# Row-tiled transposes of q and k into two PSUM banks, with a new order table, in a fused linear-attention and gMLP kernel

## The chip, the cores and the metric

The kernel runs on one core of a Trainium2 chip. The metric is device time in microseconds (us). A core has five engines that run side by side, each through its own instruction queue in order: TensorE (PE, with weight loads shown as PEld), VectorE (DVE), ScalarE (ACT), GpSimd (POOL) and SyncE (SP), which here issues the DMAs. Matrix products land in PSUM, eight banks of 128 partitions by 512 fp32 values.

## The reference

Two layers follow each other. The first is a gated linear attention over 4 batches, 8 heads, 768 positions and head size 48; the second a gated MLP with a spatial product.

```python
for t in range(S):                                   # attention, per batch b and head h
    state = alpha[:, :, t, :, None] * state + einsum('bhd,bhe->bhde', k[:, :, t], v[:, :, t])
    y[:, :, t] = einsum('bhd,bhde->bhe', q[:, :, t], state)
x = y.transpose(0, 2, 1, 3).reshape(B, S, H * D)     # 4 x 768 x 384
h = maximum(x @ w_in, 0)                             # 384 x 1024
u, v = h[..., :512], h[..., 512:]
v_n = (v - mean(v)) / sqrt(var(v) + 1e-6)            # over the last axis
v_s = einsum('ts,bsd->btd', w_spatial, v_n) + b_spatial[None, :, None]
out = (u * v_s) @ w_out                              # 512 x 384
```

## The kernel before

The 768 positions of a batch are cut into 6 chunks of 128, so there are 24 chunks, numbered `i` = 0 to 23. Inside a chunk the recurrence is turned into matrix products: cumulated logs of alpha (`cum`), k divided by and q multiplied with their exponentials (`kt`, `qt`), transposes of both (`trk`), masked scores (`sc`, then `m`), and the chunk's output `y` from scores times v and from q times the state of the chunk before. `upd`, `z`, `S` and `sb` carry the state on.

Chunks 0 to 7 are worked on as four pairs (`pair`), whose loads bring two chunks in one DMA of 384 KB. Chunks 8 to 23 are single (`first`), with loads of 192 KB. Each load is for one of alpha, k, q, v and is named `ac`, `kc`, `qc`, `vc`.

The second layer follows batch by batch: `xs`, `xt`, `xe` bring `y` into the transposed bf16 tile `xT`; `v` (`second_v`) and `u` (`second_u`) are the two halves of `x @ w_in`, `bn`, `rs`, `vn` normalise `v`, `s` is the spatial product (groups of six matmuls of 384 columns), `g` the gate, `o` the output product, `st` the store. The weights come in six loads of 768 KB: `w_in.1` (the half for `v`), `w_in.0`, `w_sp.0` to `w_sp.2`, `w_out`, each cast to bf16 by three or four `cast` operations.

All of this is first described as a list of operations with an engine, a cost for the planner and dependencies; nothing is issued at that time. The order comes from a planner and is written out as a string, `PLAN` (lines 57 to 107). A word such as `P474` says: operation 474 is issued now, on PE (`P`), DVE (`D`), ACT (`A`), POOL (`G`) or by SP (`S`; `Q` marks the end of its DMA). So the table fixes both the engine of each operation that has a choice and the order in each engine's queue. Numbers after colons are columns of extra matmuls on a constant tile `junk`, put in front of the operation; they compute nothing and keep PE active early in the run. `replay` (line 110) reads the table.

PSUM banks are handed out by `bank` in strict turn, eight of them. A bank that comes round again is written only when the engine that reads its last content has done so.

For a single chunk `tr_qk` (line 681) takes one bank as 128 x 1024 bf16 and fills it with eight transposes of 128 x 128: four of k (line 685) and four of q (line 687), each with the whole identity as the moving operand. One copy (`ev_qk`, lines 196 or 198, on ACT or DVE) brings the 128 x 1024 values to `kqT` in SBUF. The scores (line 717) use 48 rows of it, starting at row 0 or 64, so they already run as two row tiles, into two banks. Pair chunks have transposes of their own (line 480), which the change leaves alone.

Of the kernel before, what the change touches and what calls it, by code (L numbers as in the profile page):

```python
# [36 lines left out]
class Slot:  # L37
# [8 lines left out]
    "sb": {"POOL": 0.73, "DVE": 0.95},  # L46
    "vn": {"DVE": 0.42},
    "xe": {"ACT": 0.4},
    "ev": {"DVE": 0.61, "ACT": 0.91},
    "u": {"ACT": 0.39, "DVE": 0.49},  # L50
    "o": {"ACT": 0.4},
}
# [2 lines left out]
LETTERS = {"P": "PE", "D": "DVE", "A": "ACT", "G": "POOL", "S": "SP", "Q": "DMA"}  # L55

PLAN = """
G32 S34 Q33 S36 G0 S38 S94 Q35 D1 Q37 S40 A42 D2 Q39 S98 P43:512:512:192 P53:64 A44 A45 D46 Q95 S96 A54 A55 G56
P49:352 D57 Q41 D47 S100 P61:320 P59 D50 P51 A102 D62 D60 Q99 D52 S163 P241:352 P103 P113 A58 G48 P71 A104 P63 D72
Q97 A114 S165 A105 D65 A64 A115 D73 G66 A242 Q101 S167 D107 P74:512:160 D117 P111 G116 D106 A112 Q164 S169 P119:384  # L60
D75 P109 P121 A110 D68 D122 A120 G69 Q166 D76 S4 P131:352 A118 G108 D132 P134:128 G67 P123 D133 A171 Q168 S301 G70
D136 P77 A124 P172 D125 A78 P182 D135 A173 G126 Q170 P81 S9 P79 A183 P137 D128 G175 A82 D127 P138 A174 P83 G3 A184
Q5 S305 P142 A80 D176 A139 D185 G129 P180:320 A84 P178 P140 A143 D186 A177 G187 P144 D181 P190 A141 Q302 P188 D179
A145 P192 D191 A189 A6 G8 D194 D7 P200 Q10 P197 G130 S14 P146 D199 A309 S303 P88 D198 A147 D201 P85 A193 A89 G195
D202 P310 Q306 S307 A86 G196 P157 D90 A311 P203 A312 D148 A158 Q15 P204 P208 G12 P320 A205 D13 P243 A321 P206 D11
A209 D159 P153 S18 A207 P210 A322 P212 D314 Q304 S361 A211 D87 A160 P318 P215 G16 A213 D324 P221 Q308 G17 A216 D154
P151 A91 D319 G323 P225 S22 D217 A244 A222 Q19 S363 P231 G313 A226 D214 P227 A152 P149 A228 D162 P155 D92 A150 D232
P316 A218 P326 P229 Q362 A315 G325 S365 D327 P328 A317 D93 P223 D220 A156 Q23 P330 D329 S401 A224 D219 A230 P338 D20
G21 D332 A331 A369 P233 D161 G333 P341 D234 P235 G334 Q364 S405 D335 P245 D339 P253 G336 D340 Q366 P254 S403 G24
D342 P370 P257 Q402 G25 A371 D343 S436 P237 A372 A374 P258 D236 G373 Q406 D375 P239 S367 P246 G337 A240 Q404 P249  # L70
D247 S440 A238 P250 D255 G248 P377 Q437 A409 D259 S407 P269 A378 D251 G256 P270 Q368 S468 P410 D271 P344 A412 A411
Q441 P383 S438 A345 P348 G413 D385 P261 A349 Q408 P265 A414 S26 P346 D415 P262 A347 Q469 G376 D384 P350 S470 P266
G252 A351 P417 A444 Q439 S472 P379 G260 P386 D418 P445 A387 Q27 D380 P273 G416 S442 D263 A447 A446 P274 G272 D267
A449 P423 D450 P388 G381 P355 D275 A389 G382 P352 D425 G448 D424 Q471 P419 S563 P395 A353 P399 A476 G268 D354 Q473
A356 P426 S474 P397 G276 A400 D420 D357 A427 P452 Q443 S565 A396 G421 P477 P428 D453 P390 A478 G29 Q564 A429 S567
D31 G479 P458 D30 A398 P430 A28 D460 Q475 S595 G264 A480 P277 A431 D481 Q566 G422 P281 A391 S597 D459 A451 P483 Q568
A278 P285 S599 D484 A282 G482 A571 P461 D392 Q596 A286 S569 P485 A358 P454 P572 D455 A462 Q598 P289 D487 S601 A574
A573 G456 P463 D486 P393 G457 Q600 A464 S630 P293 A576 D432 G575 A290 P488 Q570 A294 D577 S634 P465 A489 D394 A603
P579 Q602 D359 S632 A466 P490 P604 D580 A433 P297 Q631 D360 A491 S670 D434 P585 A605 D435 P492 A606 A298 Q635 G607
D587 S706 A608 P505 A467 D609 P499 G578 Q633 S636 D586 A493 P501 A494 P611 D506 Q671 S674 P581 P588 A502 D582 P503  # L80
A500 D495 Q707 G583 P507 S738 A638 P515 G610 D612 Q637 A496 P639 S710 P511 A641 D497 A589 P613 D498 A640 Q675 P519
D584 S672 A643 P590 G642 P516 A504 D644 Q739 A591 P508 S708 D517 P512 D614 Q711 G518 P646 D509 S742 P520 D513 A647
G615 P527 Q673 D521 S832 G510 P617 A714 P652 D618 A678 Q709 P535 G514 S676 D619 P528 Q743 P679 G616 D529 S740 P531
A680 D653 P532 G522 A681 A683 Q833 S712 P715 D684 P620 G682 A716 P523 D654 Q677 A717 A719 S836 P536 G718 A746 P592
A645 Q741 D537 S864 A621 G530 P747 D533 A593 P655 D720 Q713 P622 S834 P686 A656 D594 A623 P524 Q837 A748 P648 S868
P657 A750 P722 D649 A687 D525 P624 G650 Q865 S744 D751 G651 P539 A658 D723 Q835 A840 S866 G538 P692 A540 P728 D694
A685 P659 Q869 G526 A625 S838 D693 P543 A660 G749 Q745 P688 S899 P547 A544 D689 A661 D729 P695 G690 Q867 S939 P662
D730 G691 A696 P753 A548 Q839 P697 A663 G721 S903 P841 D754 A698 P666 G534 A842 D626 Q900 P724 P731 S901 A872 P699
A843 A845 D725 Q940 D667 A732 G726 S870 P755 D846 A700 P664 G844 D756 A627 Q904 P733 S941 P551 A734 D757 G727 A665
P848 Q902 D629 A701 S974 G752 P873 D628 P735 D849 A874 Q871 P758 A552 S1006 D702 G876 P555 A759 Q942 A875 A877 S943  # L90
G847 P854 A556 P760 D878 P668 Q975 A761 D856 S905 P559 A703 A736 D855 P762 Q1007 S945 A907 D705 P880 A669 D704 P857
Q944 A763 D881 P908 S976 P774 A560 D737 A909 P768 Q906 S978 A910 A858 P850 G911 P788 D764 A912 Q946 P859 A947 P776
S980 G879 D851 A860 D913 P772 A765 G852 Q977 D769 P770 S1010 A775 G853 D767 P915 D766 Q979 P948 S561 D916 P792 A950
A949 P882 A773 P789 Q981 G951 S1008 A771 P777 D790 A952 P793 G914 Q1011 D883 S545 D778 P861 G884 D953 Q562 G885 P886
A862 S1012 D794 P921 Q1009 P780 S541 A982 D888 G779 A1014 P955 D887 P784 Q546 G791 A956 D922 P917 P785 Q1013 D918
P983 D923 P889 Q542 P781 A890 P796 A984 D782 A985 P891 A987 P797 G986 A954 D988 P924 A892 P804 D786 G919 A925 P1015
D863 G989 P957 P926 A1016 G795 P805 A927 D798 P961 A1018 D958 G1017 P928 D962 P990 D806 G959 P937 D963 G787 A991
P800 D1019 P801 G783 A929 D920 P1021 A938 G807 P992 D802 P893 A1022 D993 P964 G803 A894 P996 P1023 A965 D895 G994
P812 G1020 P966 D998 P808 G995 A967 D997 A896 P935 G960 P968 D898 A936 D1024 G799 A809 P816 D1025 A813 P999 S814
A817 D930 P931 A1000 S810 P1026 A969 S549 D932 P1001 Q815 P820 A1027 D970 A1002 Q811 P1028 P824 A1029 Q550 A971  # L100
P1003 A821 D973 P1038 A1004 S822 P1036 S291 A825 P1030 A1039 S279 D1037 Q823 S283 P1040 D972 A1031 Q292 D897 S287
P1042 D1005 A1041 Q280 P1044 S826 P1056 Q284 D1032 S295 P828 Q288 A1033 P1052 Q827 A829 D1034 P933 Q296 D1035 S830
P1064 A934 S553 P1045 A1043 S818 Q831 P1053 S299 P1057 Q554 S557 D1054 P1060 D1046 Q819 P1065 D1058 Q300 P1048 D1066
Q558 P1049 D1055 P1072 D1050 P1073 D1047 P1068 G1051 D1059 P1061 G1067 P1069 D1074 P1075 D1062 D1070 P1079 G1063
A1076 D1071 P1083 S1077 A1080 P1099 S1081 A1084 P1087 D1100 Q1078 S1085 P1095 S1101 A1088 Q1082 P1091 D1096 S1089
Q1086 S1097 A1092 Q1102 S1093 Q1090 Q1098 Q1094
"""


# [13 lines left out]
def kernel(  # L123
# [12 lines left out]
    nc = tc.nc  # L136
# [178 lines left out]
    def k_window(t, hp, first):  # L315

        return t[:, 3 * hp + first:3 * hp + first + 2, :].rearrange("p b d -> p (b d)")
# [285 lines left out]
    def first(i):  # L603
# [75 lines left out]
        hold = {}  # L679

        def tr_qk(_):
            pt = bank([128, 512])
            t = hold["t"] = pt.bitcast(BF16).rearrange("p (n t) -> p n t", n=8)
            for hp in range(HP):
                nc.tensor.transpose(t[:, hp, :], k_window(kt3, hp, 1), ident)  # L685
            for hp in range(HP):
                nc.tensor.transpose(t[:, HP + hp, :], qt[:, hp].rearrange("p s d -> p (s d)"), ident)  # L687

        def ev_qk(eng):
            st["kqT"] = work.tile([128, 2, HP, C], BF16, name="kqT", bufs=4).rearrange("p a h c -> p (a h) c")  # L690
            copy(eng, st["kqT"], hold["t"])

        sl = Slot(ring)
        op(("trk", i), "PE", 0.46, tr_qk, got(("kt", i), ("qt", i), ("y", i - WK)), prio=P + 5, take=sl, cols=1024)
        op(("ev", i), ENGINES["ev"], None, ev_qk, got(("trk", i), ("y", i - WK), ("sc", i - WK)),
           prio=P + 6, use=[sl])

        if not last:
            def upd(_):
                st["tp"] = bank([128, HP, D])  # L700
                for hp in range(HP):
                    for s in range(2):
                        nc.tensor.matmul(  # L703
                            out=st["tp"][:, hp, :], lhsT=k_window(kt3, hp, 2 - 2 * s),
                            rhs=st["vb"][:, 2 * hp + s, :], start=(s == 0), stop=(s == 1))

            st["sl_t"] = Slot(ring)
# [11 lines left out]
                        start=True, stop=True)  # L719

        sl0, sl1 = Slot(ring), Slot(ring)
        op(("sc", i), "PE", 0.34, sc, got(("ev", i)), prio=P + 7, take=[sl0, sl1], cols=384)

        def mk(s):
            def emit(_):
# [387 lines left out]
```

## Time and profile before

| | us |
|---|---|
| median of 5 runs | 146.99 |
| lowest, highest | 146.33, 149.19 |
| the profiled execution | 149.19 |
| its span, first to last instruction | 147.4 |
| busy: PE, DVE, ACT, POOL | 139.2, 122.4, 108.5, 84.9 |

The profile is of one execution, the slowest of the five. Its span is 1.8 us shorter than its time; the rest lies around the instructions. A matmul's length in it includes the pipeline's tail, so consecutive matmuls overlap in the rows, and the cost of one in a stream is the distance between two starts. A granted clock of 1.00 is full speed.

### The profile page before, as it was taken

The numbers are of one execution on the slowest core, as the hardware profiler recorded it, in microseconds if no ns is written. First come the engines' busy times: TensorE is split into PE (matmuls) and PEld (weight loads), VectorE is DVE, ScalarE is ACT, GpSimd is POOL, SyncE is SP. The second block draws the span as 40 slices with busy tenths as digits, with TensorE's granted clock in tenths as the row PEclk, the third lists the DMA queues.
The fourth block names the chain that finished last, engine by engine and source line by source line (L and its number), as shares of the span: only waits on it lengthen the run. The fifth ranks groups of instructions, "written<-read, shape, count | busy, mean of one in ns | idle before, by whom it ended". The sixth has DMA issues, their size and how long they took to land.

```text
span 147.4 us, 4462 instructions
## 1 busy us (share of the span) xinstructions
PE 139.2 (94%) x1700; PEld 90.5 (61%) x1713; DVE 122.4 (83%) x266; ACT 108.5 (74%) x268; POOL 84.9 (58%) x145
## 2 busy tenths in 40 slices
PE   7989989699999999999999999999999999999990
PEld 3546667255776776576666576666667576656560
DVE  6867997778998779989899897999987999575970
ACT  3456787679955976999995899999767697953051
POOL 6634655549248799844357969870694979000530
PEclk9999999789999999999999999999999999999999
DMA  4999999999999999999999998997995000479035
GB/s 115 266 261 261 265 244 336 257 318 290 319 168 207 141 272 165 197 192 171 195 190 172 189 177 155 206 188 146 196 226 139 4 0 2 165 271 342 29 139 184
DMA packets 88998, 28.61 MB, mean 194 GB/s; under 512 B 83728, under 2 KB 87440, under 8 KB 88976
## 3 DMA queue, kind: packets, MB, share of 16 engines
q1 hardware_dynamic: 88944, 28.32, 88.6%
q8 instruction: 13, 0.21, 0.7%
q14 instruction: 9, 0.07, 0.2%
q0 software_dynamic: 32, 0.00, 0.0%
HBM read 23.60 MB, written 4.72 MB: 192 GB/s over the span
## 4 chain that ended last, share of the span: by engine, by line
PE 76%; SPq 11%; DMA 6%; ACT 2%; DVE 1%; issue 1%; DVEq 0%; ACTq 0%
PE bank L791 54%; SPq L410 11%; DMA raw_w<-in_moe_w_in_dram 6%; PE bank L717 3%; PE bank L365 2%; PE bank L687 2%; PE bank L685 2%; PE bank L745 2%; PE bank L635 2%; PE bank L739 2%; PE bank L703 2%; PE bank L801 1%; PE bank L638 1%; PE bank L579 1%; PE bank L430 1%
## 5 line engine op out<-in xcount | busy, mean ns | idle before, releaser
L791 PE MATMUL bank<-w_spT,vn 128*128 128x384 bf16 x192 | 36.7, 326 | 0.0
L946 POOL TENSOR_TENSOR gT<-vsb,uT 128x384 bf16<-128x384 f32 x27 | 25.0, 940 | 15.9 <-DVE vsb L933 15.6
L791 PEld LDWEIGHTS <-vn 128*128 128x128 bf16 x192 | 17.0, 97 | 9.1 <-issue 0.2
L659 POOL TENSOR_TENSOR kt<-kc,binv 128x384 bf16<-128x384 f32 x16 | 14.6, 916 | 13.0 <-ACT bc L654 8.3
L728 DVE TENSOR_TENSOR ptm<-bank,mask 128x512 bf16<-128x512 f32 x32 | 20.9, 682 | 0.8 <-PE bank L717 0.8
L791 PE MATMUL bank<-w_in,xT 128*128 128x512 bf16 x59 | 18.2, 403 | 2.3 <-ACT w_in L196 1.2
L933 DVE TENSOR_TENSOR vsb<-bank,bsp_bc 128x384 f32<-128x384 f32 x31 | 16.2, 550 | 4.4 <-PE bank L791 4.2
L336 POOL TENSOR_TENSOR state<-state,bc 128x192 f32<-128x192 f32 x20 | 10.5, 525 | 15.0 <-DVE state L331 6.1
L791 PE MATMUL bank<-xT,w_in 128*128 128x384 bf16 x96 | 19.0, 326 | 0.1
L791 PE MATMUL bank<-w_out_sb,gT 128*128 128x384 bf16 (+1 forms) x100 | 18.6, 319 | 0.1
L852 DVE BATCH_NORM_STATS2 stats<-v_sb 128x6 f32<-128x512 bf16 x20 | 13.7, 683 | 2.1 <-ACT v_sb L202 2.1
L202 ACT ACTIVATE v_sb<-bank 128x512 bf16<-128x512 f32 x20 | 11.9, 601 | 3.0 <-PE bank L791 2.9
L196 ACT COPY xT<-bank 128x384 bf16<-128x384 bf16 x24 | 11.7, 494 | 2.1 <-PE bank L365 1.9
L196 ACT CAST x_sb<-bank 128x384 bf16<-128x384 f32 x24 | 11.7, 488 | 1.7 <-PE bank L745 1.4
L198 POOL CAST sbd<-state 64x192 bf16<-64x192 f32 x34 | 11.7, 345 | 1.8
L186 PE MATMUL bank<-junk 128*128 128x512 f32 (+7 forms) x26 | 11.7, 559 | 1.1 <-DVE junk L232 1.1
L198 DVE COPY kqT<-bank 128x512 bf16<-128x512 bf16 (+1 forms) x21 | 11.0, 544 | 1.8 <-PE bank L687 1.2
L791 PEld LDWEIGHTS <-gT 128*128 128x128 bf16 x100 | 9.0, 97 | 5.4 <-issue 0.2
L196 ACT COPY kqT<-bank 128x1024 bf16<-128x1024 bf16 (+1 forms) x11 | 9.0, 823 | 4.3 <-PE bank L687 2.5
L202 ACT ACTIVATE uT<-bank 128x384 bf16<-128x384 f32 x25 | 11.6, 494 | 0.4 <-PE bank L791 0.4
L791 PEld LDWEIGHTS <-w_in 128*128 128x128 bf16 x96 | 8.5, 97 | 4.9
L563 DVE TENSOR_TENSOR ptm<-bank,mask 128x512 bf16<-128x512 f32 x16 | 10.2, 682 | 1.2 <-PE bank L552 1.2
(126 smaller groups left out, 296.3 us busy)
## 6 DMA issues: line engine op xcount, KB each, us to landing
ac<-in_alpha_dram SPq DMA_DIRECT2D x16, 192.0 KB, 4.7
kc<-in_k_dram SPq DMA_DIRECT2D x16, 192.0 KB, 4.5
qc<-in_q_dram SPq DMA_DIRECT2D x16, 192.0 KB, 4.6
vc<-in_v_dram SPq DMA_DIRECT2D x16, 192.0 KB, 4.4
raw_w<-in_moe_w_spatial_dram SPq DMA_DIRECT2D x3, 768.0 KB, 5.9
out_dram<-raw_w SPq DMA_DIRECT2D x11, 192.0 KB, 2.1
out_dram<-o_sb SPq DMA_DIRECT2D x9, 192.0 KB, 2.0
ac<-in_alpha_dram SPq DMA_DIRECT2D x4, 384.0 KB, 6.2
```

The costliest lines, as they stand in the source:

```text
L186: nc.tensor.matmul(out=flat[:, 0:cols].rearrange("p (a b) -> p a b", a=4), lhsT=junk, rhs=junk[:, None, 0:n].to_broadcast([128, 4, n]), st ...
L196: nc.scalar.copy(out=out, in_=in_)
L198: ENG[eng].tensor_copy(out=out, in_=in_)
L202: nc.scalar.activation(out=out, in_=in_, func=AF.Relu)
L336: ENG[eng].tensor_tensor(out=st["state"], in0=st["state"], in1=st["bc"][:, :, None].to_broadcast([128, HP, D]), op=ALU.mult)
L410: nc.sync.dma_start(out=t.rearrange("p h a d -> p h (a d)"), in_=src[b, :, t0:t0 + 2 * C, :].rearrange("h (p a) d -> p h (a d)", a=2))
L659: ENG[eng].tensor_mul(out=k_blocks(kt3)[:, :, :, 0:D], in0=quad(st["kc"]), in1=st["binv"])
L728: nc.vector.tensor_tensor(out=st["ptm"][:, s], in0=st[f"pt{s}"], in1=mask4, op=ALU.mult)
L791: return lambda ps: nc.tensor.matmul(out=out(ps), lhsT=lhsT(), rhs=rhs(), start=start, stop=stop)
L852: nc.vector.bn_stats(out=stats, in_=d["v_sb"][:, tt, :])
L933: nc.vector.tensor_tensor(out=hold["vs"], in0=ps[:, 0:TH], in1=bsp_bc[:, th, :], op=ALU.add)
L946: ENG[eng].tensor_tensor(out=bt[b]["gT"][:, dsl, cols], in0=hold["vs"], in1=bt[b]["uT"][:, dsl, cols], op=ALU.mult)
```

## The change

The transposes of a single chunk are cut at partition 64. For each of the eight blocks, the upper 64 rows are transposed with the upper-left 64 x 64 of the identity into one bank, and the lower 64 rows with the lower-right part into a second bank. Each of the sixteen transposes has 64 moving columns and uses 64 of PE's rows. Each bank then holds 128 x 512 bf16 values, and one copy for each bank writes its half of the columns of `kqT`; the two copies are operations of their own, which may be on different engines. The scores wait for both.

```diff
-    "ev": {"DVE": 0.61, "ACT": 0.91},
+    "ev": {"DVE": 0.34, "ACT": 0.48},
...
         def tr_qk(_):
-            pt = bank([128, 512])
-            t = hold["t"] = pt.bitcast(BF16).rearrange("p (n t) -> p n t", n=8)
-            for hp in range(HP):
-                nc.tensor.transpose(t[:, hp, :], k_window(kt3, hp, 1), ident)
-            for hp in range(HP):
-                nc.tensor.transpose(t[:, HP + hp, :], qt[:, hp].rearrange("p s d -> p (s d)"), ident)
-
-        def ev_qk(eng):
-            st["kqT"] = work.tile([128, 2, HP, C], BF16, name="kqT", bufs=4).rearrange("p a h c -> p (a h) c")
-            copy(eng, st["kqT"], hold["t"])
-
-        sl = Slot(ring)
-        op(("trk", i), "PE", 0.46, tr_qk, got(("kt", i), ("qt", i), ("y", i - WK)), prio=P + 5, take=sl, cols=1024)
-        op(("ev", i), ENGINES["ev"], None, ev_qk, got(("trk", i), ("y", i - WK), ("sc", i - WK)),
-           prio=P + 6, use=[sl])
+            for r in range(2):
+                hold[r] = bank([128, 512]).bitcast(BF16).rearrange("p (n t) -> p n t", n=16)[:, 0:2 * HP, :]
+            for n in range(2 * HP):
+                hp = n % HP
+                for r in range(2):
+                    rows = slice(64 * r, 64 * r + 64)
+                    nc.tensor.transpose(
+                        hold[r][:, n, :],
+                        k_window(kt3[rows], hp, 1) if n < HP else qt[rows, hp].rearrange("p s d -> p (s d)"),
+                        ident[rows, rows])
+
+        sls = [Slot(ring), Slot(ring)]
+        op(("trk", i), "PE", 0.24, tr_qk, got(("kt", i), ("qt", i), ("y", i - WK)), prio=P + 5, take=sls, cols=512)
+        for r in range(2):
+            def ev_qk(eng, r=r):
+                if "kqT" not in st:
+                    st["kqT"] = work.tile([128, 2, HP, C], BF16, name="kqT", bufs=4).rearrange("p a h c -> p (a h) c")
+                copy(eng, st["kqT"][:, :, 64 * r:64 * r + 64], hold[r])
+
+            op(("ev", i, r), ENGINES["ev"], None, ev_qk, got(("trk", i), ("y", i - WK), ("sc", i - WK)),
+               prio=P + 6, use=[sls[r]])
...
-        op(("sc", i), "PE", 0.34, sc, got(("ev", i)), prio=P + 7, take=[sl0, sl1], cols=384)
+        op(("sc", i), "PE", 0.34, sc, got(("ev", i, 0), ("ev", i, 1)), prio=P + 7, take=[sl0, sl1], cols=384)
```

The table `PLAN` is replaced as a whole. Read through the list of operations it changes the order in every queue and the engine of some operations. The first 21 loads of SP's queue, before and after:

```
before: ac.0 kc.0 qc.0 ac.2 vc.0 qc.2 kc.2 vc.2 ac.4 kc.4 qc.4 vc.4 w_in.1 ac.6 w_in.0 qc.6 w_sp.0 kc.6 vc.6 w_sp.1 ac.8
after:  ac.0 ac.2 kc.0 qc.0 qc.2 vc.0 kc.2 ac.4 vc.2 qc.4 w_in.1 kc.4 w_in.0 vc.4 ac.6 w_sp.0 qc.6 kc.6 w_sp.1 vc.6 w_sp.2
```

PE's queue around the first dense product, and a stretch of single chunks:

```
before: y.3 tr.q.2.0 tr.k.2.0 xt.2 xt.3 tr.q.2.1 tr.k.2.1 updq.2 sc.2.1 sc.2.0 v.0.2 v.0.1 v.0.0 cump.3.0 v.0.3
after:  y.3 tr.q.2.1 xt.2 tr.q.2.0 v.0.1 xt.3 tr.k.2.1 tr.k.2.0 v.0.0 sc.2.1 sc.2.0 v.0.2 v.0.3 updq.2 u.0.2.0

before: trk.10 cum.11 xt.9 v.1.2 sc.10 v.1.3 o.0.0 o.0.1 trk.11 o.0.2 y.10 sc.11 upd.10 cum.12
after:  trk.10 o.0.2 o.0.1 sc.10 trk.11 v.1.3 u.1.1.0 cum.12 upd.10 y.10 sc.11 u.1.0.0 xt.10 o.0.3
```

Of the operations with a choice of engine, counted over the whole table:

| operation | before | after |
|---|---|---|
| `ev` of single chunks | 10 DVE, 6 ACT (whole) | 20 DVE, 12 ACT (halves) |
| `ev` of pairs | 11 DVE, 5 ACT | 7 DVE, 9 ACT |
| `u` evictions | 7 DVE, 25 ACT | 18 DVE, 14 ACT |
| `g` | 4 DVE, 27 POOL | 2 DVE, 29 POOL |
| `sb` | 3 DVE, 17 POOL | 2 DVE, 18 POOL |
| weight casts | 6 DVE, 2 ACT, 8 POOL | 3 DVE, 4 ACT, 9 POOL |
| `vb` of single chunks | 4 ACT, 12 POOL | 8 ACT, 8 POOL |

The matmuls on `junk` have 4,160 columns in all in both tables, in other places. On POOL the load of the spatial bias now follows the building of the masks.

## The prediction

> **What bounds the kernel now.** I read the page first, then the chain in order of time, then the windows by stage, and last TensorE's and SP's timelines around the changed step. From the page, busy times and the granted clock:
>
> ```profile
> PE 139.2 (94%) x1700; PEld 90.5 (61%) x1713; DVE 122.4 (83%) x266; ACT 108.5 (74%) x268; POOL 84.9 (58%) x145
> PEclk9999999789999999999999999999999999999999
> ```
>
> TensorE is the fullest engine, but its busy time includes matmuls on `junk`. The chain shows where real dense work begins:
>
> ```profile
> 14.93 2.52 SPq L410
> 17.50 8.60 DMA raw_w<-in_moe_w_in_dram
> 26.11 0.63 ACT w_in L196
> 26.78 0.91 PE bank L791 x3
> 27.91 2.34 PE bank L791 x5
> ```
>
> So the run is two stages. Until 26.78 us the first dense product `v` waits for the first half of `w_in`, the thirteenth load in SP's queue. Right after it five 512-column matmuls take 2.34 us, 0.47 each, where later ones take 0.22: this is the dip in the PEclk row. Then comes the PE-bound stage (columns: stretch, length, busy times of PE, PEld, DVE, ACT, POOL, clock, DMA share, GB/s):
>
> ```profile
> 60.00:75.00 15.00, 14.78 (x172) 9.70 (x172) 13.93 (x31) 14.54 (x43) 7.82 (x14) 1.00 1.14 190
> 75.00:90.00 15.00, 14.89 (x178) 9.84 (x178) 13.82 (x28) 12.48 (x32) 11.02 (x16) 1.00 1.05 180
> 90.00:105.00 15.00, 14.89 (x190) 10.15 (x191) 13.72 (x31) 14.72 (x46) 9.43 (x17) 1.00 1.03 178
> ```
>
> PE is idle about 0.1 us in 15, and DVE (92%) is close behind. Summing PE's instructions by their start-to-start times (0.163 for 384 columns, 0.217 for 512, 0.44 for one `trk`), I get 95.1 us of work from the first `trk` at 48.12; the last output product ends near 144.0, so only 0.8 us was lost there. From 26.78 the sum is 113.6, so 3.6 us were lost in all, most before 48 us.
>
> **What the step costs.** PE's timeline (start, length with the pipeline's tail, what):
>
> ```profile
> 68.48 0.39 PE L685 MATMUL bank<-ident,kt 128*128 128x128 bf16 x4
> 68.71 0.39 PE L687 MATMUL bank<-ident,qt 128*128 128x128 bf16 x4
> 68.93 0.33 PE L365 MATMUL bank<-ident,x_sb 128*128 128x128 bf16 x3
> 69.36 0.81 PE L791 MATMUL bank<-w_out_sb,gT 128*128 128x384 bf16 x4
> 70.11 0.40 PE L717 MATMUL bank<-kqT 48*128 48x128 bf16 x8
> 70.43 0.82 PE L791 MATMUL bank<-w_in,xT 128*128 128x512 bf16 x3
> 79.46 0.62 PE L717 MATMUL bank<-kqT 48*128 48x128 bf16 x16
> 80.01 1.15 PE L791 MATMUL bank<-w_spT,vn 128*128 128x384 bf16 x6
> ```
>
> Eight full transposes take 0.44 us (68.48 to 68.93, less 0.01). The scores L717 are already two row tiles: 16 take 0.55 to the next start, 8 take 0.32, so 8 more cost 0.22, 27.5 ns each where one 128-column matmul streams 53. They do overlap in pairs. But a group of them has a fixed price: the four matmuls at 69.36 end streaming at 70.01 and L717 starts at 70.11, and its own 0.22 ends at 70.33 while the next starts at 70.43. That is 0.1 on entry and 0.1 on exit.
>
> **What the Trainium skill says.** "TensorEngine Tiling (Array Packing)", Key Properties: a change of tiling mode drains the array. The trace agrees: the 0.2 us just read. Its Gotcha 1 says row tiles need different PSUM banks and raise PSUM pressure; the change uses two banks, and the orders take 285 banks in rotation of eight, against 269. "TensorE: Matmul & The Clock Gate", What you observe and What's actually happening: the clock is at half rate after an idle window of about 3.4 us; the windows show 0.50 from 28 to 30 us. The same page gives a floor of about 25 ns between matmul starts; two row tiles at L579 start 32 matmuls in 0.42 us (49.88 to L717 at 50.30), 13 ns each. The measurement decides, so 64-column transposes need not meet that floor.
>
> **The change part by part.**
>
> *Transposes.* Eight of 128 columns become sixteen of 64 columns in two tiles. Scaling L717's 27.5 ns for 128 columns gives 13.5; with the 2.5 ns above pure streaming, (26.7+2.5)/2 = 14.6, so 16 x 14.6 = 0.233 us. Saved: 16 x (0.437 - 0.233) = 3.3 us. The switch is paid by unbroken run, not by instruction. In the old order the scores of single chunks form 12 runs; in the new order `trk` and `sc` together form 18 (`sc.10 trk.11` share one, `trk.10` stands alone), and pair work has one more. 7 x 0.2 = 1.4 us. Net: -1.9 us on the path. Bounds: -3.3 if transposes pay no switch, +1.8 if tiles run one after another (16 x 29 ns = 0.467 per chunk).
>
> *Copies.* Rows of the groups view:
>
> ```profile
> L198 DVE COPY kqT<-bank 128x1024 bf16<-128x1024 bf16 x10 | 6.8, 684 | 1.3 <-PE bank L687 1.2
> L196 ACT COPY kqT<-bank 128x1024 bf16<-128x1024 bf16 x6 | 6.1, 1021 | 2.5 <-PE bank L687 2.5
> L198 DVE COPY kqT<-bank 128x512 bf16<-128x512 bf16 x11 | 4.2, 416 | 0.4 <-PE bank L480 0.3
> L196 ACT COPY kqT<-bank 128x512 bf16<-128x512 bf16 x5 | 2.8, 585 | 1.7 <-PE bank L480 1.7
> ```
>
> Half copies of 128x512 exist for the pairs. The new order puts 20 halves on DVE and 12 on ACT: 20 x 0.416 + 12 x 0.585 = 15.3, against 12.9. Neighbours on an engine overlap (two `vn` of 0.432 take 0.74), so about +1 us, spread over two engines. The order also moves 11 `u` evictions (0.55 each) from ACT to DVE and takes weight casts, `sb` and `g` off it: DVE's total rises by about 1.2 us, POOL's by 1.7, ACT's hardly. None is on the path by itself. What waits is `sc`, now on two copies, and everything behind it in PE's queue. I take +0.5 us of new PE waits, from 0 to +5 (the rival below).
>
> *Start.* SP's own timeline shows about 1.44 us per pair load, paced by the transfers:
>
> ```profile
> 13.45 1.44 SPq L410 DMA_DIRECT2D qc<-in_q_dram  x1
> 17.50 1.46 SPq L1037 DMA_DIRECT2D raw_w<-in_moe_w_in_dram  x1
> ```
>
> The new order issues `w_in.1` eleventh, before `kc.4` and `vc.4`, so at 13.45 instead of 17.50. The same 8.6 us to landing gives 22.1; by bytes queued up to its end (4.7 MB at the rates of the GB/s row: 20.1, plus the 3.0 by which the old one was late against that reckoning) 23.1. I take 22.5, 0.9 for its two casts in a row on DVE, and start `v` at 23.4: 3.4 earlier. But `tr.k.2`, `xt.3`, `sc.2` and `updq.2` now come after `v`: 0.44 + 0.17 + 0.43 + 0.5 and a switch, 1.75 us of PE work moved behind. Net -1.6. What else moves in the queues: `kc.0`, `qc.0`, `vc.0` and `vc.2` are one place (0.6 to 1.5 us) later, `kc.4` and `vc.4` two; the bias load follows the masks on POOL, so `bb.1` and the transposes behind it wait until about 10 us; `w_sp.0` still waits on SP for the casts of `w_in.1`. Pair 1's `y` should end near 21.5, so 1.9 us of slack cover these. Without that cover each tenth late costs a tenth. `junk` is again 4,160 columns, elsewhere; PE still idles before `v`, so I count the clock dip as unchanged (0, or -1.8 if it vanishes).
>
> *Loads of single chunks.* They were issued 7 to 20 us before use and landed about 4.6 us after issue. Remaining PE work puts the new `trk.8` and `trk.10` at the old times and `trk.23` 4 us earlier, where the slack was over 4: no cost. The tail after the last product is unchanged.
>
> Sum: -1.9 + 0.5 - 1.6 = -3.0 us. The profiled execution took 149.19 (span 147.4 and 1.8 around it) and would take 146.2; it was 2.2 slower than the median of five, so I set the difference against the median: 146.99 - 3.0 = 144.0.
>
> **Rivals.**
> (a) The start pays fully: `v` comes a microsecond earlier, the clock dip goes, no new waits. 144.0 - 0.5 - 1.8 = 141.7. For: PEclk dips only there. Against: the same idle gap ahead of `v`.
> (b) The start gives nothing, because pair 1 or 2 is late instead of the weight. 144.0 + 1.6 = 145.6. For: three of their loads move back. Against: the slack above.
> (c) Tiles don't overlap in transposes: 16 x 0.233 more, 147.7. Against: L717 and L579.
> (d) Slower: DVE takes over as the bound from 48 to 120 us:
>
> ```profile
> 48.00:120.00 72.00, 71.30 (x893) 48.19 (x901) 64.33 (x133) 62.02 (x162) 50.74 (x79) 1.00 0.95 170
> ```
>
> It was busy 64.3 of 72 us (0.89). With about 2.2 more (the half copies and `u` that fall there) beside 69.9 us of PE (72 less 3.3, plus 6 switches) it would need 0.95, more than in any stretch above. If its in-order queue, waiting for PE, ACT and POOL at every step, holds only 0.88, the stretch takes 66.5/0.88 = 75.6: 146.99 + 3.6 + 0.2 (the switch outside) - 1.6 = 149.2. It decides below a share of about 0.90. For: 92% at 60 to 75 with ACT at 97%. Against: waits are short and PE hid nearly all of them.
>
> **Numbers.** Forecast 0.60 (own range 142.2 to 145.5), (a) 0.12, (b) 0.10, (c) 0.05, (d) 0.13. The measurement tells about 1% from no change. Faster by over 1%: forecast, (a) and a third of (b), 0.75. Within 1%: the rest of (b), (c) and a little of (d), 0.12. Slower: 0.13. The range takes in (a) with 0.9 of the other early losses gone too, (b), and (c) with the 0.5 of new waits, and leaves out (d): 140.8 to 148.2.
>
> **What would show it.** Right: `v` starts between 22.5 and 24.5; an isolated `trk` spans about 0.43 us start to start with its switches and one beside `sc` about 0.23; half copies near 0.42 and 0.59; PE idle under 0.2 us in 15. Wrong: transposes 29 ns apart; PE waits on kqT, or DVE above 95% with PE gaps; `v` held by `xT`.

## The result and the profile after

| | before | after |
|---|---|---|
| median | 147.11 (75 runs) | 146.48 (38 runs) |
| lowest, highest | 146.33, 149.19 | 146.14, 148.13 |
| a profiled execution at full clock: time, span | 146.7, 144.9 | 146.4, 144.7 |

The ratio is 0.9968, interval 0.9955 to 0.9982. The changed kernel is 0.3% faster, 0.6 us by the medians, where 3.0 us were forecast. It is faster by more than chance, but far less than forecast.

One thing must be known to read the numbers: in some executions the granted clock falls to half for a few microseconds near the start of the run, which costs about 1.5 us, and the first profile of before was one of these, so a second profile of before at full clock (`before_look`, 146.7 us) serves for the comparison below.

The page of after, busy times and granted clock:

```profile
PE 135.5 (94%) x1837; PEld 88.0 (61%) x1849; DVE 121.9 (84%) x276; ACT 108.6 (75%) x271; POOL 86.6 (60%) x148
PEclk9999999999999999999999999999999999999999
```

The share of PE is the same 94%, and the clock row has no dip (nor has that of `before_look`). The start of the first dense product `v`: first PE's timeline in `before_look`, then SP's and PE's timelines of after (start, length, what, idle time ahead and what ended it).

```profile
25.50 2.19 PE L791 MATMUL bank<-w_in,xT 128*128 128x512 bf16 x9 [0.48 <-ACT w_in L196]
```

```profile
13.36 1.44 SPq L1044 DMA_DIRECT2D raw_w<-in_moe_w_in_dram  x1
...
23.30 0.33 PE L593 MATMUL bank<-sbd,kqT 128*128 128x96 bf16 x4 [0.25 <-POOL sbd L199]
23.46 0.39 PE L481 MATMUL bank<-ident,qt 128*128 128x128 bf16 x4
23.68 0.33 PE L366 MATMUL bank<-ident,x_sb 128*128 128x128 bf16 x3
23.85 0.39 PE L481 MATMUL bank<-ident,qt 128*128 128x128 bf16 x4
24.08 0.81 PE L798 MATMUL bank<-w_in,xT 128*128 128x512 bf16 x3
```

The weight is issued at 13.36, as forecast (13.45), and lands 8.2 us later, at about 21.5. But `v` starts at 24.08, and it has no wait of its own: it stands in PE's queue behind `y.3` (23.30), the end of pair 1's attention, and behind `xt.2` and two groups of pair 2's transposes. In `before_look` it waited for the cast of the weight, and `y.3` started at 21.23. The casts of the weight in after, on DVE and POOL:

```profile
22.62 0.90 DVE L199 CAST w_in<-raw_w 128x512 bf16<-128x512 f32 x2
23.31 0.68 POOL L199 CAST w_in<-raw_w 128x512 bf16<-128x512 f32 x1
```

They start a microsecond after the landing, because both stand in their queues behind pair 1's state (`state` on DVE at 22.35, `sbd` on POOL at 22.26). The last ends at 23.99, just before `v`. So pair 1 stands ahead of `v` in PE's queue, and also ahead of the casts that `v` reads.

The new transposes and copies, PE's timeline and the groups (busy us and mean ns behind the bar):

```profile
58.79 0.29 PE L689 MATMUL bank<-ident,kt 64*128 64x64 bf16 x8
58.91 0.30 PE L689 MATMUL bank<-ident,qt 64*128 64x64 bf16 x8
59.13 1.48 PE L798 MATMUL bank<-w_out_sb,gT 128*128 128x384 bf16 x8
```

```profile
L197 ACT COPY kqT<-bank 128x512 bf16<-128x512 bf16 x21 | 11.8, 595 | 4.8 <-PE bank L481 2.4
L199 DVE COPY kqT<-bank 128x512 bf16<-128x512 bf16 x27 | 10.6, 412 | 0.7 <-PE bank L481 0.6
```

Eight transposes take 0.12 us from start to start, so 15 ns each and 0.24 for sixteen; then 0.10 for the switch until the next product starts. The halves take 0.41 and 0.60. All of this is as forecast.

The PE-bound stage, by windows (stretch, length, busy times of PE, PEld, DVE, ACT, POOL, clock, DMA share, GB/s):

```profile
60.00:75.00 15.00, 14.25 (x196) 9.24 (x197) 13.29 (x33) 13.66 (x41) 8.12 (x13) 1.00 0.98 176
75.00:90.00 15.00, 14.89 (x242) 10.12 (x242) 13.93 (x30) 13.37 (x34) 13.14 (x20) 1.00 1.03 187
90.00:105.00 15.00, 14.95 (x191) 9.62 (x189) 13.70 (x34) 14.53 (x45) 7.77 (x14) 1.00 1.00 176
```

PE is idle 0.11 and 0.05 us in the last two, but 0.75 in the first.

To see where time is lost I add to each start of a `trk` the PE work that is left at that place (start-to-start times, as in the prediction; an estimate, good to some tenths of a microsecond). A sum that stays level means that PE lost nothing in between; where it rises, that much was lost.

| kernel | PE work in all | at first `v` | trk.8 | trk.11 | trk.12 | trk.23 |
|---|---|---|---|---|---|---|
| before_look | 124.4 | 139.1 | 140.7 | 140.8 | 140.8 | 141.0 |
| after | 122.5 | 137.5 | 139.3 | 139.7 | 140.5 | 140.9 |

After starts 1.6 ahead, loses as much as before until trk.8 (1.8 against 1.6), then loses 1.6 where before loses 0.3, half of it in one place between trk.11 and trk.12. At trk.23 it is level with before.

### The profile page after: what moved, and what is told of

Same layout as the page of the kernel before. It is cut to its first block, busy times and chain, and to the rows that moved or that the text cites. A ratio compares the mean times of both kernels' runs of the same rounds, so it can differ in the third digit from the quotient of the medians.

```text
span 144.7 us, 4767 instructions
## 1 busy us (share of the span) xinstructions
PE 135.5 (94%) x1837; PEld 88.0 (61%) x1849; DVE 121.9 (84%) x276; ACT 108.6 (75%) x271; POOL 86.6 (60%) x148
## 4 chain that ended last, share of the span: by engine, by line
PE 69%; DVE 11%; ACT 7%; POOL 3%; DMA 3%; issue 3%; SPq 0%; POOLq 0%; DVEq 0%; ACTq 0%
PE bank L798 47%; DMA ac<-in_alpha_dram 3%; PE bank L724 3%; PE bank L689 3%; PE bank L187 2%; DVE ptm L735 2%; PE bank L366 2%; DVE vn L891 2%; PE bank L752 2%; ACT binvp L439 2%; DVE ptm L564 2%; PE bank L636 2%; ACT bank L448 2%; PE bank L553 2%; PE bank L710 1%
## 5 line engine op out<-in xcount | busy, mean ns | idle before, releaser
L953 POOL TENSOR_TENSOR gT<-vsb,uT 128x384 bf16<-128x384 f32 x29 | 26.4, 928 | 15.5 <-DVE vsb L940 14.9
L798 PE MATMUL bank<-xT,w_in 128*128 128x384 bf16 x96 | 19.9, 326 | 0.0
L798 PE MATMUL bank<-w_in,xT 128*128 128x512 bf16 x60 | 17.3, 378 | 0.8 <-issue 0.2
L197 ACT COPY kqT<-bank 128x512 bf16<-128x512 bf16 x21 | 11.8, 595 | 4.8 <-PE bank L481 2.4
L187 PE MATMUL bank<-junk 128*128 128x512 f32 (+7 forms) x34 | 12.0, 453 | 2.1 <-DVE junk L233 1.1
L199 POOL CAST sbd<-state 64x192 bf16<-64x192 f32 x36 | 12.6, 350 | 1.9
L891 DVE TENSOR_SCALAR vn<-v_sb,mvs,rstd 128x512 bf16<-128x512 bf16 x24 | 10.7, 475 | 1.9 <-ACT rstd L884 1.9
L197 ACT COPY xT<-bank 128x384 bf16<-128x384 bf16 x24 | 11.2, 483 | 1.3 <-PE bank L366 1.0
L199 DVE COPY kqT<-bank 128x512 bf16<-128x512 bf16 x27 | 10.6, 412 | 0.7 <-PE bank L481 0.6
```

The costliest lines, as they stand in the source:

```text
L187: nc.tensor.matmul(out=flat[:, 0:cols].rearrange("p (a b) -> p a b", a=4), lhsT=junk, rhs=junk[:, None, 0:n].to_broadcast([128, 4, n]), st ...
L197: nc.scalar.copy(out=out, in_=in_)
L199: ENG[eng].tensor_copy(out=out, in_=in_)
L798: return lambda ps: nc.tensor.matmul(out=out(ps), lhsT=lhsT(), rhs=rhs(), start=start, stop=stop)
L891: nc.vector.tensor_scalar(out=d["vn"][:, t, :], in0=d["v_sb"][:, t, :], scalar1=d["mvs"][:, t, 0:1], scalar2=d["rstd"][:, t:t + 1], op0=AL ...
L953: ENG[eng].tensor_tensor(out=bt[b]["gT"][:, dsl, cols], in0=hold["vs"], in1=bt[b]["uT"][:, dsl, cols], op=ALU.mult)
```

## The experiments

In the order tables only the moved items are shown. Times are medians, ratios are to the kernel before.

**The kernel before, looked at again.** No edit.

> The kernel before once more, unchanged, for a second profile. Theory A: the first profile, 149.2 us, showed an execution with a clock dip that the usual one of 147.1 lacks; here the span is about 145.3, the granted clock stays at 1.00 from 27 to 32 us, the first dense product v still starts near 26.8 behind the weight load, and the last output product ends near 141.8 instead of 144.0. Theory B: the usual execution has the dip too, and is shorter because the first weight lands earlier: v starts near 24.5.

It took 146.7 us, span 144.9, clock 1.00 throughout, `v` at 25.50 instead of 26.78. So 1.28 us of the late start in the first profile belonged to that execution. (The weight landed at 24.8 here and at 26.1 in the first profile. In tiles_old_order and tiles_old_two, which have the same load order, `v` starts at 26.06 and 25.64, so the usual start may be some tenths later than 25.50.) Theory A was right that the dip is missing, and wrong that `v` would still start near 26.8.

**One half of the change at a time.** Tiles and half copies in the old order (each whole copy replaced by two halves on its engine; four instructions moved by a place or two), and the new table with whole transposes (one copy at the place and engine of the later half):

```diff
 tiles_old_order: code of after
-PLAN of after
+PLAN of before, ev.i -> ev.i.0 ev.i.1 on the same engine
 whole_new_order: code of before
-PLAN of before
+PLAN of after, ev.i.0 ev.i.1 -> one ev.i
```

> Only the tiled transposes and the two half copies, with the old order table (each half copy on the engine that had the whole one, one after the other; four instructions moved by a place or two so that a bank is not handed out too early). trk and sc then form 28 runs of row tiles among single chunks instead of 12. Theory A, the switch is paid by run: PE's sum falls from 124.4 to 124.3 us, the half copies cost up to 1 us more, 147.0 to 148.0. Theory B, the switch is not paid by transposes: 3 us less, 144.0 to 144.8.

> Only the new order table, with whole transposes into one bank and one copy (on the engine and at the place of the later half). PE's sum is 125.2 us, 2.7 more than with tiles, 0.8 more than before because scores are less often neighbours. Theory A, PE sets the time and the tiles bring what the sum says: 148.2 to 149.2. Theory B, waits of the new order set it and the tiles are hidden: 146.3 to 146.9. Theory C, the start is the gain: below 146.

whole_new_order took 149.25, ratio 1.0168 (1.0146 to 1.0191). Against after's 146.48 the tiles bring 2.8 us at this order, where the sums of PE work (125.2 and 122.5) say 2.7: the term of the transposes is right, and the gain passes to the end in full. The order alone costs 2.4 us (the kernel before took 146.87 beside it); it loses 1.3 us from trk.8 to trk.23, so most of after's new waits come with the order and not with the halves. This is Theory A, at the end of its range.

tiles_old_order took 150.78, ratio 1.0255 (1.0228 to 1.0281): 3.9 us slower than the kernel before (146.87 beside it) with no more PE work (124.3). I had expected nothing like it. So each half of the change alone makes the kernel slower, and only the two together make it faster. Two places in PE's timeline, 8 and 3 matmuls that want a bank:

```profile
85.38 0.20 PE L689 MATMUL bank<-ident,kt 64*128 64x64 bf16 x1
86.19 0.27 PE L689 MATMUL bank<-ident,kt 64*128 64x64 bf16 x7 [0.61 <-DVE vsb L940]
...
109.04 0.81 PE L798 MATMUL bank<-w_in,xT 128*128 128x512 bf16 x3 [0.49 <-DVE vsb L940]
```

The first transpose goes out into its bank at 85.38; the second, which wants the second bank, waits 0.61 until DVE's `vsb` has emptied it. With one bank more per chunk, each bank comes round sooner, and in the old order it isn't always empty yet. PE's waits from 44 us on (total us, times, longest), of which the same view of `before_look` has none:

```profile
PE bank L689 <- DVE vsb L940: 0.6, 1, 0.6
PE bank L798 <- DVE vsb L940: 0.5, 1, 0.5
PE bank L798 <- DVE qt L670: 0.4, 1, 0.4
```

The waits for `vsb`, 1.1 us, are for a bank. The third is probably one too, since `qt` also reads a bank. This is PSUM pressure, as the Trainium skill ("TensorEngine Tiling (Array Packing)", Gotcha 1) warns without a size. These waits are less than half of the 3.9 us; 0.56 more is a later start of `v` in the profiled execution (26.06), and the rest is not traced.

To see whether it is how long the bank is held, the second half of each copy went to the other engine:

```diff
-D ev.i.0  D ev.i.1   (or A, A)
+D ev.i.0  A ev.i.1   (or A, D)
```

> The run tiles_old_order (tiles and half copies in the old order, both halves on one engine, one after the other: 150.78), with the second half on the other of DVE and ACT. Theory A (the second bank, held until the second of two copies of one engine is done, is what costs the old order its time): the banks come free 0.4 to 0.6 us sooner per chunk, 148.3 to 149.8 us. Rival B (the bank more at each take is what costs, however long it is held, or the copies now fall into the other engine's busy stretches): 150.3 to 152 us.

It took 153.39, ratio 1.0445 (1.0421 to 1.0469), 2.6 more. Two stretches of windows, tiles_old_order and then tiles_old_two (PE's busy time is the first after the length; 15.00 in `before_look`):

```profile
75.00:90.00 15.00, 14.27 (x191) 8.59 (x189) 12.48 (x25) 11.53 (x30) 11.57 (x17) 1.00 1.13 190
```

```profile
75.00:90.00 15.00, 13.54 (x181) 8.29 (x181) 12.69 (x28) 10.92 (x28) 11.72 (x17) 1.00 1.04 184
```

So this is no remedy. But it doesn't test the hold, because the banks were held hardly less long: from a chunk's first transpose to the end of its last copy 1.53 us in the mean, where tiles_old_order has 1.60 and Theory A wanted 0.4 to 0.6 less. The second copy now stands in the other engine's queue. How much of the 3.9 us is the extra bank and how much the place of the copies in their queues is left open.

**The weight's load.** In the kernel before, `w_in.1` goes eleventh, and nothing else moves; in after, it goes back behind `vc.4`.

```diff
 win_early (before)
-S: ac.4 kc.4 qc.4 vc.4 w_in.1
+S: ac.4 kc.4 w_in.1 qc.4 vc.4
 after_win_late (after)
-S: qc.4 w_in.1 kc.4 w_in.0 vc.4 ac.6
+S: qc.4 vc.4 kc.4 w_in.1 w_in.0 ac.6
```

> The kernel before with one change: on SP the first w_in load is issued eleventh instead of thirteenth, ahead of q and v of pair 2. Theory A, the load gates the first dense product and the rest is ready: v starts 2 to 3 us earlier, but pair 2's transposes, scores and state products stand ahead of v in this order and now come later, so 146.0 to 147.2. Theory B, the weight alone sets the start: 144.5 to 145.5. Theory C, the loads pushed back decide: 147.5 to 149.

> The changed kernel; only on SP, w_in.1 and w_in.0 are issued behind vc.4 and kc.4, the place of w_in.1 in the kernel before. It prices the early load of the weight in the new table. Theory A (the weight, issued at about 17, lands at about 24.8 as before, so the first product starts at 25.4 or later): 1.3 to 2 us slower, 147.7 to 148.5 us. Rival B (pair 1 sets the start whichever way, the early load is worth little): the first product before 24.6, 146.4 to 147.0 us.

win_early took 147.50, ratio 1.0046 (1.0028 to 1.0065): slower, though the weight was early, as Theory C has it. Its chain of waits, from the late load to `v`:

```profile
15.52 8.48 DMA vc<-in_v_dram
24.02 0.51 ACT vbp L196
...
25.83 0.64 PE bank L552 x32
26.47 0.32 PE bank L791
```

`vc.4`, pushed back, is what `v` now waits for: 26.47. The transfers run back to back, so a load brought forward pushes others back, and in the old PE order pair 2's `sc` and `updq` stand ahead of `v`. after_win_late took 147.90, ratio 1.0070 (1.0040 to 1.0099), and its median over the executions at full clock is 147.31; `v` started at 25.20 there, after 1.20 us of waiting for the weight's cast. So in the new table the early load is worth 1.4 us by the medians, as Theory A has it, and 0.9 at full clock. That it pays there and not in the old order fits the table, which also puts pair 2's work behind `v`; this was not tried by itself.

**Pair 1, which `v` now stands behind.** Two ways to bring it forward:

```diff
 after_vc_early
-S: qc.0 qc.2 vc.0 kc.2 ac.4 vc.2 qc.4
+S: qc.0 vc.0 qc.2 kc.2 vc.2 ac.4 qc.4
 after_queues
-A: ebcp.0 ev.q.1.0 ev.q.1.1     G: S.0 ktp.1.1     D: z.0 ktp.1.0
+A: ev.q.1.0 ev.q.1.1 ebcp.0     G: ktp.1.1 S.0     D: ktp.1.0 z.0
```

> The changed kernel; only on SP, vc.0 is issued ahead of qc.2 and vc.2 ahead of ac.4, so that the values of pairs 0 and 1 go one place earlier. Theory A (the first w_in product starts late because pair 1 is late, and pair 1 is late because vc.0 lands at 12.0): updq.0 at about 12.2 instead of 13.57, the first w_in product at 23.0 to 23.4 instead of 24.08, and the gain reaches the end: 145.5 to 146.1 us. Rival B (whatever is moved back takes its place: ac.4 is then issued at 10.2 instead of 8.7): the first product at 23.8 to 24.4, 146.3 to 147.0 us.

> The changed kernel with the loads as they are; three engines take pair 1's work ahead of what waits for updq.0: on ACT ev.q.1.0 and ev.q.1.1 ahead of ebcp.0, on POOL ktp.1.1 ahead of S.0, on DVE ktp.1.0 ahead of z.0. Theory A (vc.0 makes pair 1 late only through these queues): sc.1 at 15.7 to 17 instead of 18.29, the first w_in product at 22.9 to 23.5 instead of 24.08, 145.4 to 146.1 us. Rival B (pair 1 is late by its own loads, ac.4 and vc.2): sc.1 earlier, updq.1 still at 20, the first product at 23.9 to 24.2, 146.3 to 146.7 us.

after_vc_early took 149.82, ratio 1.0170 (1.0123 to 1.0217), and neither theory had it. My reason was wrong: not `vc.0` but `qc.2` is what the chain needs next, since PE's queue has pair 1's q transposes ahead of pair 0's scores. Its chain, and the clock:

```profile
5.72 6.21 DMA qc<-in_q_dram
...
12.05 1.03 DVE qt L460 x2
...
13.84 0.35 PE bank L553 x16
...
PEclk9999559999999999999999999999999999999999
```

`sc.0` (L553) comes at 13.84 instead of 12.64. PE is idle longer ahead of it, and in this kernel the clock is at half rate in most of 15 to 22 us, so the price of the delay is more than the delay. The one execution of six at full clock took 147.86.

after_queues took 146.24, ratio 0.9955 (0.9942 to 0.9969), 0.2 better than after; `v` came at 23.70 instead of 24.08, but trk.8 started no earlier (48.06 against 48.04). The time lies between the two theories, nearer to Rival B. What pair 1's chain consists of is seen in after's chain of waits:

```profile
12.64 0.35 PE bank L553 x16
...
15.41 1.12 PE bank L187 x2
16.53 0.22 PE bank L481 x4
16.76 0.49 PE bank L187 x2
17.25 0.22 PE bank L481 x4
...
17.73 0.63 PE bank L187 x2
18.36 0.38 PE bank L553 x16
18.76 2.28 DVE ptm L564 x4
```

Three pieces of L187, the matmuls on `junk`, stand between the transposes and the scores of pair 1. I took these out (1,024 of 4,160 columns, in a kernel that also has the queue orders of after_queues and the two edits on DVE shown below):

```diff
-P: tr.k.1.0:512 tr.k.1.1:256 sc.1.0:256
+P: tr.k.1.0 tr.k.1.1 sc.1.0
```

> The run after_m10_evq_queues (145.72) without the junk columns in front of tr.k.1.0 (512), tr.k.1.1 (256) and sc.1.0 (256), which compute nothing and which the chain of the changed kernel shows between pair 1's operations. Theory A (pair 1 sets the start, and these stand in its way): the first w_in product at 22.6 to 23.3 instead of 23.55, and as a wait ahead of trk.8 keeps part of it, 145.2 to 145.6 us. Rival B (PE is then idle longer between 14 and 19 us and the granted clock falls, as in after_vc_early): a 5 in the PEclk row and 147 to 149 us. Rival C (loads and DVE's masks set pair 1's pace): 145.6 to 145.9 us.

It took 146.82, ratio 0.9987 (0.9968 to 1.0007), 1.1 slower than with them (145.72): Rival B's fall of the clock, at a time just under its range. Windows of PE's idle time and what follows (first number after the length is PE's busy time, the clock is third from the end):

```profile
16.00:18.00 2.00, 0.05 (x5) 0.02 (x4) 1.96 (x5) 1.50 (x3) 1.36 (x5) 0.64 1.17 305
18.00:20.00 2.00, 2.00 (x36) 1.60 (x37) 1.85 (x4) 0.00 (x0) 1.47 (x4) 0.50 1.10 346
20.00:22.00 2.00, 2.00 (x30) 1.53 (x30) 1.16 (x2) 0.86 (x3) 0.00 (x0) 0.50 1.12 333
```

DVE is full (1.96 of 2.00) and PE idle: `sc.1` waits 1.95 us for a copy on DVE, behind masks and state, and so starts at 17.98 with the `junk` gone, no earlier than with it (17.76 in after_m10_evq_queues). The `junk` was not in the way but filled the wait and kept the clock up. Without it the clock fell to 0.50, and `v` came at 25.70 instead of 23.55.

**The loss between trk.11 and trk.12.** PE's and then DVE's timeline of after there:

```profile
63.32 0.33 PE L746 MATMUL bank<-sbd,kqT 128*128 128x96 bf16 x4 [0.38 <-DVE ptm L735]
```

```profile
60.98 0.69 DVE L735 TENSOR_TENSOR ptm<-bank,mask 128x512 bf16<-128x512 f32 x1 [0.32 <-PE bank L724]
61.59 1.08 DVE L891 TENSOR_SCALAR vn<-v_sb,mvs,rstd 128x512 bf16<-128x512 bf16 x1
62.59 0.68 DVE L735 TENSOR_TENSOR ptm<-bank,mask 128x512 bf16<-128x512 f32 x1
```

`y.10` (L746) waits for the mask `m.10.0` (62.59), which stands in DVE's queue behind `vn.1.0`; and that `vn` takes 1.08 us, where a `vn` elsewhere takes 0.40. The edit puts the mask first:

```diff
-D: m.10.1 vn.1.0 m.10.0
+D: m.10.1 m.10.0 vn.1.0
```

> The changed kernel; only on DVE, the mask m.10.0 goes ahead of the normalisation vn.1.0, which there took 1.08 us instead of 0.40 and held m.10.0 and so y.10 on PE. Theory A (the 0.8 us that the stretch between trk.11 and trk.12 loses in both kernels with the new table is this collision): 0.4 to 0.8 us less, 145.7 to 146.1 us, and no wait of PE for ptm near 63. Rival B (PE is fed by other queues there that are as late): 146.4 to 146.6 us.

It took 145.80, ratio 0.9943 (0.9922 to 0.9963): 0.7 us less than after by one swap, Theory A. DVE's timeline and the window:

```profile
60.87 1.29 DVE L735 TENSOR_TENSOR ptm<-bank,mask 128x512 bf16<-128x512 f32 x2 [0.32 <-PE bank L724]
62.07 0.48 DVE L891 TENSOR_SCALAR vn<-v_sb,mvs,rstd 128x512 bf16<-128x512 bf16 x1
```

```profile
60.00:75.00 15.00, 14.91 (x203) 9.53 (x201) 13.26 (x35) 14.23 (x42) 8.26 (x14) 1.00 1.02 176
```

The same `vn`, half a microsecond later, takes 0.48, PE is idle 0.09 us instead of 0.75, and trk.12 starts 5.33 us after trk.11 instead of 5.92.

**Further waits ahead of trk.8.** PE waits at 39.66 for the copy `ev.q.3.0`, which is behind statistics on DVE; that edit, and then all together:

```diff
 after_m10_evq, on top of after_m10
-D: bn.0.5 ev.q.3.0
+D: ev.q.3.0 bn.0.5
 after_m10_evq_queues: and the three moves of after_queues
```

> The changed kernel with m.10.0 ahead of vn.1.0 on DVE, as in the run after_m10 (145.80), and the copy ev.q.3.0 ahead of the statistics bn.0.5 on DVE, where PE waits 0.57 us at 39.66 for it before sc.3.0. Theory A (this wait is the one that swallows what is gained before 39 us): trk.8 0.4 to 0.6 us earlier, 145.1 to 145.5 us. Rival B (vn.0.4 and vn.0.5 come later with bn.0.5 and PE waits for them, or another wait ahead of trk.8 takes its place): 145.6 to 146.0 us.

> The run after_m10_evq with the queue order of after_queues as well (ev.q.1.0, ev.q.1.1 ahead of ebcp.0, ktp.1.1 ahead of S.0, ktp.1.0 ahead of z.0), which alone brought the first w_in product from 24.08 to 23.70 and yet trk.8 no earlier. Theory A (the wait before sc.3.0 had swallowed it): a further 0.2 to 0.4 us, 144.8 to 145.2 us. Rival B (swallowed by pair 2's own loads): the same time as after_m10_evq to 0.1.

after_m10_evq took 146.09, ratio 0.9951 (0.9927 to 0.9975): nothing gained. `sc.3.0` no longer waits, but the next products wait 0.28 us for `w_spT` on ACT and 0.25 for another copy to `kqT`, and from the first `v` to trk.8 it takes 23.9 us as in after_m10 (`v` itself came 0.6 later in this execution). With all edits it is 145.72, ratio 0.9922 (0.9903 to 0.9940), the lowest median here, but not told apart from after_m10. Only the swap on DVE is shown to be worth something; the stretch ahead of trk.8 fills up again whichever single wait is taken out.

## Why the prediction was wrong

It forecast 3.0 us and 0.6 came by the medians (0.2 by the two spans, for `before_look` is 0.4 faster than the median of before; a usual `v` some tenths after 25.50 would explain that, but it is not shown). The step that failed is the start: "start `v` at 23.4: 3.4 earlier", for a net gain of 1.6. The runs showed 1.4 earlier, for a net loss of 0.3. By the prediction's own terms, with the sums of the table above:

| term | forecast | measured |
|---|---|---|
| transposes less switches | -1.9 | -1.9 by PE work |
| start: `v` earlier, work moved behind it | -1.6 | +0.3 |
| new waits of PE | +0.5 | +1.5 (0.2 ahead of trk.8, 1.3 after) |

- *Transposes and switches: right.* 0.24 us for sixteen against 0.233, a switch of 0.10; the two kernels with the new table differ by 2.8 us where their work differs by 2.7. Behind the first `v` the traces have 15 runs of row tiles before and 23 after, of which single chunks 12 and 18, as reckoned. Rival (c) is out.
- *Copies: right in size* (0.41 and 0.60 against 0.416 and 0.585). DVE did not become the bound (rival d): it is busy 13.3 to 13.9 of 15 us, as before.
- *Start: the largest error, 1.9 us.* The step failed at both ends. The starting point, 26.78, was that of an execution 2.2 us above the median; at full clock it is 25.50 (1.28 us of the error). The end point was 24.08 instead of 23.4 (0.68), for "1.9 us of slack cover these" was wrong. The weight landed even earlier than reckoned (21.5 against 22.5), but pair 1's `y`, reckoned to end near 21.5, started at 23.30, and the casts of the weight stood behind pair 1 too. That is the mechanism of rival (b). Only 1.4 us came, and 1.75 us of PE work had gone behind `v`. Why pair 1 is 2.1 us later than in `before_look` is shown for 0.4 of it (after_queues); the rest is open.
- *The transfer to the median failed with it.* The prediction noted that the profile was 2.2 us above the median and still subtracted a difference worked out inside it. A difference may be carried over only if its terms are the same in both executions; the wait for the weight wasn't. Counting the dip "as unchanged (0, or -1.8)" was right for the usual execution for a reason it did not give: there is no dip in it to lose, before or after.
- *New waits: a third of the size, and in the wrong place.* The forecast put them on `sc` and its copies; they came mostly from the new order, and 0.6 to 0.8 of the 1.6 us after trk.8 is one collision of `vn` on DVE, which the durations of before don't show: no `vn` on DVE took more than 0.78 us there, and half of them 0.41 or less.
- The sign "PE idle under 0.2 us in 15" holds in two windows of three, and the third led to the collision of `vn`. The signs "`v` starts between 22.5 and 24.5" (24.08) and "half copies near 0.42 and 0.59" held. They look at the kernel after alone, so they could not show that the start of `v` to subtract from, 26.78, was too late.

What is left of the waits after trk.8 (about 1.0 in after_m10 against 0.3 in before_look) and the share of the 3.9 us of tiles_old_order are not traced further.

## What to carry to other kernels

Take a profile that stands well above the median for what it is: work out differences from an execution that looks like the median, or ask of each term whether it would be there in it. When a load is brought forward, reckon the second thing the consumer needs with the same care as the load, and follow what its in-order queue holds ahead of it. A narrower operation that needs one more buffer may lose in the old order, as it did here; price it with the order it will run in, not alone.

## What the runs showed of the hardware

- A `vn` of 128 x 512 bf16 on DVE takes 0.41 us in the median, and 1.08 beside two gate products on POOL (60.73 to 62.52); it took 1.05 beside POOL's `kt` and weight casts at 35.65, and 0.98 to 1.05 at the same two places in whole_new_order. The Trainium skill says why ("SBUF — State Buffer", Who interferes with whom): DVE's fast two-port form of this operation shares a port pair with POOL, the one that issues first holds it for its whole instruction, and the other blocks. The traces agree: in after `vn` ends at 62.67, 0.15 us after POOL's second product (62.52, POOL's spans being rough). In after_m10, where it starts half a microsecond later, at 62.07, it ends at 62.55, again 0.15 after that product (62.40), and takes 0.48. Here the price was not `vn` itself but the mask queued behind it.
- Sixteen 64 x 64 transposes in two row tiles start 15 ns apart, as forecast from the scores.
- The clock fell while PE had been busy for more than half of the time. Windows of after_all_less_junk around the fall and the return:

```profile
16.00:16.50 0.50, 0.03 (x1) 0.00 (x0) 0.46 (x2) 0.50 (x2) 0.03 (x2) 1.00 1.35 281
16.50:17.00 0.50, 0.00 (x0) 0.00 (x0) 0.50 (x2) 0.50 (x1) 0.48 (x1) 0.54 1.21 272
23.00:23.50 0.50, 0.50 (x40) 0.50 (x34) 0.50 (x3) 0.45 (x2) 0.30 (x1) 0.63 1.21 305
```

It fell at about 16.5, only half a microsecond into the wait before `sc.1`, and came back at 23.4, so it stayed at half rate for 6.8 us. In the 3.4 us ahead of the fall PE was busy 2.4 (the matmuls' tails counted). The other two falls in the profiles are alike: busy 2.1 of 3.4 us ahead of 14.9 in after_vc_early, half rate to 21.7; busy 2.3 of 3.4 ahead of 27.4 in the first profile of before, half rate to 30.8. The Trainium skill ("TensorE: Matmul & The Clock Gate", What's actually happening) names an idle window of about 3.4 us as what brings half rate. The lengths, once and twice 3.4 us, fit such a window, but PE did not have to be idle for all of it: its longest single gap ahead of a fall was 1.2 us. No threshold comes out of these runs, for after_win_late was busy only 2.1 of 3.4 us from 22.0 and kept its clock in the profiled execution. With the 1,024 `junk` columns gone, the mean clock was 0.976 to 0.988 in all 14 executions; with them it was 0.997 to 1.000 in all six.
